# The third piece of a weight load moved to the scalar engine's DMA queue, an unused small transfer left out, and another load cut in two

## The chip, the cores and the metric

The kernel runs on one core of a Trainium2 chip. The metric is the device time of one execution in microseconds (us); the time before is the median of three runs.

## The reference

Two blocks are computed from the same input `x` (2048 tokens of 512 numbers, bf16) and mixed by a gate per token:

```python
x = A_x
g = _sigmoid((x * gate_w).sum(-1, keepdims=True))
a = _A_ref(x, A_wqkv, A_wo)
b = _B_ref(x, B_w1, B_w3, B_w2)
return g * a + (1 - g) * b

# _A_ref: linear attention, 32 heads of 16
q, k, v = qkv[0], qkv[1], qkv[2]                       # from x @ wqkv
phi = lambda t: jnp.where(t > 0, t + 1, jnp.exp(t)) + 1e-6
pq, pk = phi(q), phi(k)
kv = jnp.einsum("bhsd,bhse->bhde", pk, v)
z = jnp.einsum("bhsd->bhd", pk)
num = jnp.einsum("bhqd,bhde->bhqe", pq, kv)
den = jnp.einsum("bhqd,bhd->bhq", pq, z)[..., None] + 1e-6
o = num / den                                          # then o @ wo

# _B_ref: SwiGLU with F = 1376
h = _silu(x @ w1) * (x @ w3);  out = h @ w2
```

## The kernel before

The 2048 tokens are cut into 16 tiles of 128 (`t`), and these into four blocks of four (`tb`). The 512 input columns are cut into four pieces of 128, numbered `kc` = 0 to 3, which are the contraction steps of every projection.

**Loads.** All large loads are issued by SyncE (SP, `dq = nc.sync`) in the order of the program, each on the queue behind the one before: the first two token tiles in natural layout (`xN`, L129), the four pieces of the joined q and k weights (`wqk[:, kc, :]`, 128 rows of 2 KB each, L126), transposed loads of the tokens from tile 2 on (`xT`, L123) with natural ones between them (L141), then the weights `wr`, `w1`, `w3`, `wv`, `wo`, `w2` and `w2x` (L143 to L156). The queue of ScalarE (ACT) carries one transfer in the whole kernel: 32 bytes of each of 384 rows of `A_wqkv` into `touch` (L133), a tile that nothing reads. Ahead of it ACT runs one activation of one column (`act_pre`, L130), whose result nothing reads either; it makes ACT load its function table at the start. The pieces of code are

```python
nc.scalar.activation(out=act_pre[:], in_=warm[:, 0:1], func=ACT.Exp)
nc.scalar.dma_start(out=touch[:], in_=wqkv_r[:, 1:KC, 0:16])
for kc in range(KC):
    load_wqk(kc)
```

Every DMA also carries one of eight completion semaphores in turn; a later DMA that gets the same one waits for the DMA that had it before.

**Opening of TensorE.** The order is written out by hand (a manual schedule). 13 warm-up matmuls on a constant (L359) run while the loads are under way. Then the first two token tiles are transposed on TensorE (L365, six blocks), and VectorE and ScalarE copy the results into `xT` (L379 to L382). Then the first four projections (k and q of tiles 0 and 1) run piece by piece, as the pieces of `wqk` arrive: `kc` 0 for all four, the last two transposes, `kc` 1 for all four, and then `kc` 2 and 3 for the two k, then for the two q (all matmuls of L183).

```python
for kc in range(2):
    for n, t in (("k", 0), ("q", 0), ("k", 1), ("q", 1)):
        first_mm(n, t, kc)
    if kc == 0:
        transpose_kc(3, bank[0])
for kc in range(2, KC):
    for t in range(2):
        first_mm("k", t, kc)
```

After that come, tile by tile, the projections of q and k, `phi` (exp on ACT, two operations on VectorE), and the product of the phi'd k with the natural tokens (L231).

**The rest.** For each block the gated unit (`glu_step`, L303 and L309, with a product on VectorE at L315), in between the denominators, and the outputs: `b_part` (L492) with `w2`, `a_part` (L475), the mix on VectorE (L498) and the store (L508). `w2` is read for the first time by L492 of block 0.

Of the kernel before, what the change touches and what calls it, by code (L numbers as in the profile page):

```python
# [8 lines left out]
ACT = mybir.ActivationFunctionType  # L9
# [3 lines left out]
BF16 = mybir.dt.bfloat16  # L13
# [3 lines left out]
def kernel(  # L17
# [17 lines left out]
    nc = tc.nc  # L35
    P = nc.NUM_PARTITIONS

    Bb, S, D = A_x.shape
# [3 lines left out]
    KC = D // P  # L42
# [4 lines left out]
    FC = F // P  # L47
# [14 lines left out]
    wqkv_r = A_wqkv.rearrange("(kc d) n -> d kc n", d=P)  # L62
# [3 lines left out]
    consts = ctx.enter_context(tc.tile_pool(name="consts", bufs=1))  # L66
# [5 lines left out]
    warm = nc.const_aps.tensor(1.0, [P, 256], BF16)  # L72
# [7 lines left out]
        out=bmask[:], in_=bmask[:], pattern=[[-Dh, HPC], [0, Dh]], compare_op=ALU.is_ge,  # L80
# [3 lines left out]
        out=bmask[:], in_=bmask[:], pattern=[[Dh, HPC], [0, Dh]], compare_op=ALU.is_ge,  # L84
# [23 lines left out]
    wqk = consts.tile([P, KC, 2 * D], BF16, name="wqk")  # L108
# [6 lines left out]
    w3 = consts.tile([P, KC, F0], BF16, name="w3")  # L115
    w2 = consts.tile([P, FC, D], BF16, name="w2")
    xT = consts.tile([P, KC, S], BF16, name="xT")
    act_pre = consts.tile([P, 1], BF16, name="act_pre")
    dq = nc.sync

    def load_xT(t):
        ts = slice(t * P, (t + 1) * P)
        dq.dma_start(out=xT[:, :, ts], in_=x2d[ts, :], transpose=True)  # L123

    def load_wqk(kc):
        dq.dma_start(out=wqk[:, kc, :], in_=wqkv_r[:, kc, 0 : 2 * D])  # L126

    x_first = x2d[0 : 2 * P, :].rearrange("(p j) d -> p j d", j=2)
    dq.dma_start(out=xN[:, 0:2, :], in_=x_first)  # L129
    nc.scalar.activation(out=act_pre[:], in_=warm[:, 0:1], func=ACT.Exp)  # L130

    touch = consts.tile([P, KC - 1, 16], BF16, name="touch")
    nc.scalar.dma_start(out=touch[:], in_=wqkv_r[:, 1:KC, 0:16])  # L133
    for kc in range(KC):
        load_wqk(kc)
    natural = {3: (2, 4), 5: (4, 8), 8: (8, 16)}
    for t in range(2, NT):
        load_xT(t)
# [3 lines left out]
    with nc.allow_non_contiguous_dma(reason="gate column"):  # L142
        dq.dma_start(  # L143
            out=wr[:, :, 2 * FR : NR], in_=gate_w.rearrange("(kc d o) -> d kc o", d=P, o=1)
# [3 lines left out]
    for w, w_r, cuts in ((w1, w1_r, (0, KC)), (w3, w3_r, (0, KC))):  # L148
# [2 lines left out]
    dq.dma_start(out=wv[:], in_=wqkv_r[:, :, 2 * D : 3 * D])  # L151
    dq.dma_start(out=wo[:], in_=A_wo.rearrange("(kc d) n -> d kc n", d=P))
    w2_r = B_w2[0:F0, :].rearrange("(fc f) d -> f fc d", f=P)
    dq.dma_start(out=w2[:], in_=w2_r)
    w2x_r = B_w2[F0:F, :].rearrange("(i r) d -> i (r d)", i=RP)
    dq.dma_start(  # L156
        out=w2x[:].rearrange("p r d -> p (r d)"),
        in_=w2x_r[None].to_broadcast([TPB, RP, RG * D]),
# [442 lines left out]
```

## Time and profile before

| what | value |
|---|---|
| median of three runs | 178.73 us (178.44 to 178.74) |
| the profiled execution's own time | 177.74 us |
| its span | 176.0 us, so 1.74 us lie around it |
| TensorE busy | 171.3 us (97%) |
| VectorE, POOL, ScalarE busy | 110.5, 63.3, 59.1 us |
| chain that ended last | PE 95%, DMA 2% |
| DMA of SP's queue, ACT's queue | 28948 packets with 15.41 MB, 400 packets with 0.01 MB |

Times are counted from the start of the span. PE is TensorE's matmuls and PEld its weight loads, SPq and ACTq are the DMA issues of SyncE and ScalarE. Matmuls overlap each other, so the start of a matmul says more than its duration: four full ones take 0.86 us of the chain.

### The profile page before, as it was taken

The numbers are of one execution on the slowest core, as the hardware profiler recorded it, in microseconds if no ns is written. First come the engines' busy times: TensorE is split into PE (matmuls) and PEld (weight loads), VectorE is DVE, ScalarE is ACT, GpSimd is POOL, SyncE is SP. The second block draws the span as 40 slices with busy tenths as digits, with TensorE's granted clock in tenths as the row PEclk, the third lists the DMA queues.
The fourth block names the chain that finished last, engine by engine and source line by source line (L and its number), as shares of the span: only waits on it lengthen the run. The fifth ranks groups of instructions, "written<-read, shape, count | busy, mean of one in ns | idle before, by whom it ended". The sixth has DMA issues, their size and how long they took to land.

```text
span 176.0 us, 2668 instructions
## 1 busy us (share of the span) xinstructions
PE 171.3 (97%) x952; PEld 82.4 (47%) x969; DVE 110.5 (63%) x207; ACT 59.1 (34%) x109; POOL 63.3 (36%) x106
## 2 busy tenths in 40 slices
PE   8999999999999999999999999999999999999993
PEld 5444444444456443444444466444444444444453
DVE  0399788888764899777343477853435775344363
ACT  4364544544753533322433101224226122422000
POOL 5087656656300668586300044540000662000000
DMA  5988969997205112323200013330000233000001
GB/s 172 277 197 207 164 123 237 403 352 231 78 4 56 22 30 41 78 63 91 58 0 0 0 34 84 84 89 0 0 4 0 60 89 89 4 0 0 30 30 60
DMA packets 29360, 15.58 MB, mean 88 GB/s; under 512 B 21156, under 2 KB 27556, under 8 KB 29348
## 3 DMA queue, kind: packets, MB, share of 16 engines
q1 hardware_dynamic: 28948, 15.41, 35.1%
q8 instruction: 7, 0.11, 0.3%
q10 hardware_dynamic: 400, 0.01, 0.1%
q14 instruction: 5, 0.04, 0.1%
HBM read 8.86 MB, written 2.10 MB: 62 GB/s over the span
## 4 chain that ended last, share of the span: by engine, by line
PE 95%; DMA 2%; issue 1%; SPq 0%; DVE 0%
PE bank L303 20%; PE bank L492 20%; PE bank L309 19%; PE bank L183 16%; PE bank L231 8%; PE bank L475 8%; PE bank L245 3%; DMA wqk<-in_A_wqkv_dram 2%; PE bank L278 2%; PE bank L447 0%; SPq L129 0%; PE bank L462 0%; DVE o L498 0%; PE bank L365 0%
## 5 line engine op out<-in xcount | busy, mean ns | idle before, releaser
L315 DVE TENSOR_TENSOR hT<-bank,sg 128x512 bf16<-128x512 f32 x40 | 27.3, 682 | 31.0 <-PE bank L309 28.9
L303 PE MATMUL bank<-xT,w 128*128 128x512 bf16 x158 | 40.8, 379 | 0.2
L309 PE MATMUL bank<-xT,w 128*128 128x512 bf16 x156 | 40.5, 379 | 0.2
L314 ACT ACTIVATE sg<-bank 128x512 bf16<-128x512 f32 x40 | 23.9, 597 | 45.9 <-PE bank L303 45.9
L492 PE MATMUL bank<-w,hT 128*128 128x512 bf16 (+2 forms) x176 | 37.0, 355 | 0.5 <-issue 0.3
L337 POOL TENSOR_TENSOR pqs<-pq,rden 128x512 bf16<-128x512 bf16 x16 | 16.9, 1057 | 54.3 <-issue 46.8
L183 PE MATMUL bank<-wqk,xT 128*128 128x512 bf16 x126 | 30.2, 379 | 0.1
L215 POOL TENSOR_TENSOR zacc<-zacc,pk 128x128 f32<-128x128 f32 x56 | 23.3, 447 | 10.4 <-DVE pk L201 10.4
L492 PEld LDWEIGHTS <-hT 128*128 128x128 bf16 x180 | 16.7, 98 | 18.4 <-issue 0.8
L309 PEld LDWEIGHTS <-w 128*128 128x128 bf16 x160 | 15.7, 98 | 18.9
L303 PEld LDWEIGHTS <-w 128*128 128x128 bf16 x160 | 15.5, 98 | 18.2 <-issue 0.2
L498 DVE SCALAR_TENSOR_TENSOR o<-bank,omg_all,aga 128x512 bf16<-128x512 f32 (+2 forms) x18 | 12.4, 692 | 14.5 <-PE bank L492 11.7
L183 PEld LDWEIGHTS <-xT 128*128 128x128 bf16 x128 | 12.5, 98 | 14.9 <-issue 0.3
L322 POOL TENSOR_TENSOR pr<-pq,zb 128x512 f32<-128x512 bf16 x16 | 18.4, 1155 | 0.1
L231 PE MATMUL bank<-pk,xN 128*128 128x512 bf16 x62 | 16.3, 379 | 0.2
L475 PE MATMUL bank<-M,pqT 128*128 128x512 bf16 x61 | 15.6, 379 | 0.1
L196 ACT ACTIVATE eq<-bank 128x512 bf16<-128x512 f32 x16 | 9.4, 597 | 16.0 <-PE bank L183 14.9
L201 DVE SCALAR_TENSOR_TENSOR pk<-bank,emk 128x512 bf16<-128x512 f32 x16 | 11.1, 692 | 1.6
L196 ACT ACTIVATE ek<-bank 128x512 bf16<-128x512 f32 x16 | 9.4, 597 | 6.5 <-PE bank L183 6.5
L201 DVE SCALAR_TENSOR_TENSOR pq<-bank,emq 128x512 bf16<-128x512 f32 x16 | 11.1, 692 | 0.5
L326 DVE TENSOR_REDUCE den<-pr 128x32 f32<-128x512 f32 x16 | 10.8, 676 | 0.0
L231 PEld LDWEIGHTS <-xN 128*128 128x128 bf16 x64 | 6.3, 98 | 7.5
(54 smaller groups left out, 95.6 us busy)
## 6 DMA issues: line engine op xcount, KB each, us to landing
w<-in_B_w_dram SPq DMA_DIRECT2D x3, 1280.0 KB, 10.3
out_dram<-o SPq DMA_DIRECT2D x15, 128.0 KB, 1.9
wqk<-in_A_wqkv_dram SPq DMA_DIRECT2D x4, 256.0 KB, 3.7
xN<-in_A_x_dram SPq DMA_DIRECT2D x1, 1024.0 KB
xN<-in_A_x_dram SPq DMA_DIRECT2D x2, 256.0 KB, 2.9
xN<-in_A_x_dram SPq DMA_DIRECT2D x1, 512.0 KB, 4.2
wv<-in_A_wqkv_dram SPq DMA_DIRECT2D x1, 512.0 KB, 11.2
wo<-in_A_wo_dram SPq DMA_DIRECT2D x1, 512.0 KB, 12.2
```

What stands on the lines that cost most here:

```text
L183: nc.tensor.matmul(ps[:], lhsT=xT[:, kc, t * P : (t + 1) * P], rhs=w[:, kc, :], start=(kc == 0), stop=(kc == KC - 1),)
L196: nc.scalar.activation(out=e[:], in_=ps[:], func=ACT.Exp)
L201: nc.vector.scalar_tensor_tensor(out=dst, in0=ps[:], scalar=0.0, in1=em[:], op0=ALU.max, op1=ALU.add)
L215: nc.gpsimd.tensor_tensor(out=(zaccb if t == NT - 1 else zacc)[:, cs], in0=zacc[:, cs], in1=pk[t][:, cs], op=ALU.add,)
L231: nc.tensor.matmul(bank[kc][:], lhsT=xN[:, t, kc * P : (kc + 1) * P], rhs=pk[t][:], start=(t == 0), stop=(t == NT - 1),)
L303: nc.tensor.matmul(g_ps[:], lhsT=w1[:, kc, fs], rhs=xT[:, kc, tok], start=(kc == 0), stop=(kc == KC - 1),)
L309: nc.tensor.matmul(u_ps[:], lhsT=w3[:, kc, fs], rhs=xT[:, kc, tok], start=(kc == 0), stop=(kc == KC - 1),)
L314: nc.scalar.activation(out=sg[:], in_=g_ps[:], func=ACT.Silu)
L315: nc.vector.tensor_tensor(out=hT[tb][:, fc, :], in0=u_ps[:], in1=sg[:], op=ALU.mult)
L322: nc.gpsimd.tensor_tensor(out=pr[t][:], in0=pq[:, t, :], in1=zb[:], op=ALU.mult)
L475: nc.tensor.matmul(ps[:], lhsT=pqT[:, c, ts], rhs=M2[:, c, :], start=(c == 0), stop=(c == KC - 1),)
L492: nc.tensor.matmul(ps[:, 0 : cs.stop - cs.start], lhsT=hT[tb][:, fc, tt * P : (tt + 1) * P], rhs=w2[:, fc, cs], start=(fc == 0 and not sta ...
```

## The change

The third piece of `wqk` (`kc` = 2) is issued on ACT's queue, the other three stay on SP's. The first activation of ACT now writes its one column into that piece, `wqk[:, 2, 0:1]`, so that the transfer, which overwrites the column, has to wait for the activation. The transfer into `touch` and the tiles `act_pre` and `touch` are left out. The load of `w2` (1280 KB) becomes two of 640 KB, one behind the other on SP's queue.

```diff
-    def load_wqk(kc):
-        dq.dma_start(out=wqk[:, kc, :], in_=wqkv_r[:, kc, 0 : 2 * D])
+    def load_wqk(kc, queue):
+        queue.dma_start(out=wqk[:, kc, :], in_=wqkv_r[:, kc, 0 : 2 * D])
...
-    nc.scalar.activation(out=act_pre[:], in_=warm[:, 0:1], func=ACT.Exp)
-
-    touch = consts.tile([P, KC - 1, 16], BF16, name="touch")
-    nc.scalar.dma_start(out=touch[:], in_=wqkv_r[:, 1:KC, 0:16])
+    nc.scalar.activation(out=wqk[:, 2, 0:1], in_=warm[:, 0:1], func=ACT.Exp)
+
     for kc in range(KC):
-        load_wqk(kc)
+        load_wqk(kc, nc.scalar if kc in (2,) else dq)
...
-    dq.dma_start(out=w2[:], in_=w2_r)
+    for a, b in ((0, FC // 2), (FC // 2, FC)):
+        dq.dma_start(out=w2[:, a:b, :], in_=w2_r[:, a:b, :])
```

More of the change, by code (lines that the diff above doesn't have):

```diff
@@ L117 @@
     xT = consts.tile([P, KC, S], BF16, name="xT")
-    act_pre = consts.tile([P, 1], BF16, name="act_pre")
     dq = nc.sync
```

## The prediction

> **What bounds the kernel now.** I read the page's chain first, to see whether anything but TensorE sets the end.
>
> ```profile
> PE 171.3 (97%) x952; PEld 82.4 (47%) x969; DVE 110.5 (63%) x207; ACT 59.1 (34%) x109; POOL 63.3 (36%) x106
> PE 95%; DMA 2%; issue 1%; SPq 0%; DVE 0%
> ```
>
> TensorE is the bound, and the only load in the chain is 2% of it. So a load matters only where TensorE stands still for it. The chain in order of time, from its start, shows where that can be:
>
> ```profile
> 1.26 3.11 DMA wqk<-in_A_wqkv_dram
> 4.37 0.04 issue
> 4.41 1.02 PE bank L183 x4
> 5.43 0.11 PE bank L365 x2
> 5.54 3.60 PE bank L183 x16
> 9.14 0.65 PE bank L231 x3
> ```
>
> The first projection starts at 4.41, when piece 0 of wqk has landed (issued 1.26, 3.11 later). From there four matmuls take 0.86 (0.215 each), and 16 should take 3.45 but took 3.60: 0.15 us of stall. The timeline of the weight loads says where:
>
> ```profile
> 4.32 0.62 PEld L183 LDWEIGHTS <-xT 128*128 128x128 bf16 x4
> 5.06 0.31 PEld L365 LDWEIGHTS <-xN 128*128 128x128 bf16 x2
> 5.33 1.23 PEld L183 LDWEIGHTS <-xT 128*128 128x128 bf16 x7
> 6.83 0.74 PEld L183 LDWEIGHTS <-xT 128*128 128x128 bf16 x4 [0.27 <-issue]
> ```
>
> Counting on from 4.41: four matmuls of kc 0 to 5.27, two transposes (0.11) to 5.38, four of kc 1 to 6.25, two of kc 2 to 6.68. The first of kc 3 should start at 6.68; the loads resume at 6.83. The four pieces are issued 0.46 apart from 1.26 on, and by the landings of the four issues, asked one by one (3.1, 3.4, 3.9 and 4.1 us later), they land at 4.37, 5.1, 6.1 and 6.8. So piece 3 is 0.15 late, piece 2 has 0.2 to spare (needed at 6.25) and piece 1 has 0.2 to 0.3 (needed at 5.38). Behind 6.83 the chain is matmul after matmul; the waits listed for SP name no xT or weight load, and the tokens of tile 2 land 4.1 after 3.15, at 7.25, for use at 8.12.
>
> **The change, part by part.** PE, DVE and POOL keep their operations in their order. What moves is in the first 7 us. ACT's opening before:
>
> ```profile
> 0.80 1.28 ACT L130 ACT_TABLE_LOAD   x1 [0.80 <-PEq L585]
> 0.86 0.43 ACTq L133 DMA_DIRECT2D touch<-in_A_wqkv_dram  x1
> 2.10 0.20 ACT L130 ACTIVATE act_pre<-const-bfloat16-1.0 128x1 bf16<-128x1 bf16 x1
> 4.08 0.28 ACT L380 ACTIVATE xT<-bank 128x128 bf16<-128x128 f32 x1 [1.78 <-PE bank L365]
> ```
>
> *The activation* writes another address, the same 128x1: 0.20 us, no change. *The new wait:* the transfer of piece 2 stood on SP at 2.20; it is now issued when the activation ends, at 2.30, say 2.35, and the issue takes 0.43 as touch's did, to 2.78. Behind it on ACT waits only the copy L380, which comes at 4.08 for another reason: 1.3 us of cover, cost nothing.
>
> *SP's queue* has one issue less between pieces 1 and 3: piece 3 is issued at 2.20 instead of 2.67, and all that follows, the xT transposes and natural tokens too, 0.46 sooner until w2. Their data come no sooner by that, since they queue behind the same bytes, but none is later. The completion semaphore that each waits for moves by one place; before, none of these waits held SP, and none comes near.
>
> *Touch left out.* Its data all fell into 0.4 us, by the DMA view of 2.9 to 3.3 and of 3.3 to 3.7 us:
>
> ```profile
> q1 hardware_dynamic: 64, 0.10, 66.0%
> q10 hardware_dynamic: 400, 0.01, 56.2%
> ...
> q1 hardware_dynamic: 79, 0.16, 103.7%
> ```
>
> SP's queue (q1) had 66% of the engines beside touch (q10) and 104% after it: 0.38 x 0.4 = 0.15 us given back, by q10's own share 0.22. Everything behind touch, pieces 0 to 3, moves up by 0.15 to 0.22. Piece 0 gains nothing by it: its first weight load is at 4.32 because L379's copy ends at 3.97 + 0.29 = 4.26, and a load takes 0.1, so 4.41 stands. Piece 3 would land at 6.58 to 6.65 instead of 6.8, ahead of 6.68. That is the whole 0.15.
>
> *When do piece 2's data enter?* The trace has no full piece on ACT's queue. Bounds: SP's first transfer was issued at 0.81 and its data began between 1.5 and 2.0 (DMA share 0.06 there, 0.69 in the next half us), about 1.1 later, so 3.45; touch was issued at 0.86 and its data came at 2.9, 2.05 later, so 4.4. A piece takes 256 KB at 404 GB/s, 0.65 us. A landing comes about 0.6 after the data (xN: data to 3.0, landed when PE went on at 3.64). So without touch kc 0's data end near 3.55 and kc 1's near 4.3. Any entry between these gives the old order, 2 behind 1 and ahead of 3. Most of 3.45 to 4.4 lies there, and I take that.
>
> A rule speaks against the idea: the Trainium skill, page "DMA: Bandwidth & Descriptors", section "Issuing engines are not separate DMA queues", says that transfers of all queues run on the same 16 engines, and a second issuer saves only issue time. By that page the sum would be 0.15 as well, all of it touch's; the trace agrees that the engines are shared (66% and 56.2% in one window).
>
> *w2 in halves* costs SP one more issue:
>
> ```profile
> 30.27 3.66 SPq L154 DMA_DIRECT2D w<-in_B_w_dram  x1
> 33.98 2.95 SPq L156 DMA_DIRECT2D w2x<-in_B_w_dram  x1
> 46.10 1.21 SPq L421 DMA_TRANSPOSE zaT<-zaccb  x1
> ```
>
> Between 0.5 us (wr's and wv's issues) and 3.66 again; nearest is the small end, as 3.66 goes with the bytes and these stay. SP then stands idle from 36.93 to 46.10, so even 3.66 is covered; uncovered it would be 3.66. w2 lands 13.5 us after 30.27, at 43.8, and L492 reads it near 68. Nothing.
>
> Sum: -0.15 us. On the profiled execution 177.74 becomes 177.59. That execution lies 0.99 under the median, which I put down to nothing here, so the difference goes onto the median: 178.73 - 0.15 = 178.58. A change under 0.2% (0.36 us) is about what a measurement of this kernel, whose three runs spread over 0.30, can't tell from none. What would be late next after 6.68 is tile 2's xT, with 0.9 to spare.
>
> **The rivals.**
>
> *Piece 2 gets in piece 1's way.* If its data enter at 3.45 and take turns with piece 1's, or go ahead of them, piece 1 comes 0.65 later, less 0.15: 5.12 + 0.5 = 5.62. Then kc 3 can start at 5.62 + 0.04 + six matmuls (1.30) = 6.96, 0.13 later than now: 178.86. For it: SP's entry delay. Against: ACT's one row says 2.05.
> The same page, section "Queues, rings and completion order", has each engine go round the queues packet by packet. By that rule this rival is right if the entry is early; in touch's window q1 kept 64 packets, so some turn-taking shows, but no two large loads are seen side by side.
>
> *Piece 2 falls behind piece 3*, entering at 4.4 or later. Then it lands where the last piece does, 6.65, and kc 3 follows two matmuls later: 6.65 + 0.04 + 0.43 = 7.12, 0.29 later: 179.02.
>
> *Slower: touch was not idle.* It reads a bit of each row of pieces 1 to 3 ahead of them. If a first reading is slow, these pieces now pay for it. The price is xN's cold start: 160 and 341 GB/s in its two half us against 397 later, 0.30 + 0.07 = 0.37 us of lost data time. One such loss puts piece 3 at 6.8 - 0.15 + 0.37 and costs 0.2; from the second on it decides: two cost 0.58, so 179.31, three 0.95, 179.68. Against it: piece 0 was not touched, and ran at 397 GB/s.
>
> *Faster by more:* touch's data came while xN's last were landing. If xN too is freed by 0.22, the transposes and everything behind start that much sooner: -0.37, 178.36. Against it: touch starts at 2.9, when most of xN is through.
>
> **How the numbers follow.** Old order 0.40, xN freed too 0.18, piece 1 delayed 0.17, piece 2 last 0.10, cold rows 0.15. The likeliest gives 178.58. Faster by over 0.36: 0.11 of the 0.18, which lies on the bound, and 0.08 for spread: 0.19. Slower by over 0.36: 0.15 and 0.08 of the two delays, which reach 0.29: 0.23. Same: 0.58. The range goes from 178.36 less 0.25 of spread, 178.1, to cold rows with two losses, 179.3. It leaves out three losses and the rest of the spread.
>
> **What the changed profile would show.** ACT's issue of wqk at 2.35 with q10 carrying 0.26 MB; piece 3's issue at 2.2; no gap of the weight loads before kc 3 (6.68) and none before kc 1 (5.38) and kc 2 (6.25). A gap before kc 1 means the first rival, before kc 2 the second, both with lower GB/s between 3.5 and 6 the third; transposes before 3.65 the fourth. A change behind 10 us, in the middle or the end, would make this prediction wrong in kind, and so would a time outside the range.

## The result, and the profile after

The changed kernel takes 179.05 us (median of 18 executions, 178.55 to 181.43), the kernel before 178.41 us (18 executions, 177.75 to 178.83). The ratio is 1.0043, with a 95% interval of 1.003 to 1.0056; two executions at 181.4, with a mean granted clock of 0.991 of full, are left out of it, so it holds nothing of what they cost. So the kernel became slower by 0.43%, 0.77 us (the two medians are 0.64 apart), where the forecast had 178.58 against 178.73, 0.15 us faster. The profiled execution took 179.00 us with a span of 177.3 us; that of before took 177.74 with 176.0.

The page of the changed kernel first, its engines and the shares of its chain:

```profile
PE 172.3 (97%) x969; PEld 82.3 (46%) x969; DVE 110.1 (62%) x207; ACT 59.2 (33%) x109; POOL 63.3 (36%) x106
PE 94%; DMA 3%; ACT 1%; DVE 0%; issue 0%
```

TensorE is still the bound, but DMA has gone from 2% to 3% of the chain, and ACT, which was not among the first, has 1%. The chain of the changed kernel in order of time (start, duration, what) shows both:

```profile
2.10 0.21 ACT wqk L129
2.31 0.02 issue
2.33 5.24 DMA wqk<-in_A_wqkv_dram
7.57 0.04 issue
7.61 2.75 PE bank L181 x12
10.36 0.65 PE bank L229 x3
```

(Lines have numbers lower by two or one: L181 was L183, L125 was L126.) Before, the chain went through piece 0 and TensorE from 4.41 on. Now it goes through the function table, the activation, and piece 2 on ACT's queue: issued at 2.33, landed 5.24 later, at 7.57. The weight loads of TensorE say where it stood still:

```profile
4.28 0.55 PEld L181 LDWEIGHTS <-xT 128*128 128x128 bf16 x4
4.95 0.31 PEld L363 LDWEIGHTS <-xN 128*128 128x128 bf16 x2
5.22 0.80 PEld L181 LDWEIGHTS <-xT 128*128 128x128 bf16 x5
7.61 0.74 PEld L181 LDWEIGHTS <-xT 128*128 128x128 bf16 x4 [1.59 <-issue]
```

Before, seven loads followed one another from 5.33 and 0.27 us of gap stood ahead of kc 3. Now the gap is 1.59 us and stands ahead of kc 2, after five loads (four of kc 1 and one for kc 2 whose matmul had to wait for its data). From 7.61 the two matmuls of kc 2 take 0.43, so kc 3 starts at 8.04; before it started at 6.83. That is 1.21 us, and the spans, 176.0 and 177.3, differ by nearly the same. So nothing behind kc 3 changed the time.

The two queues in the DMA view, from 4.2 to 5.0 us and from 5.0 to 5.5 us (packets, MB, share of the 16 engines):

```profile
q1 hardware_dynamic: 116, 0.20, 69.4%
q10 hardware_dynamic: 29, 0.06, 22.6%
...
q10 hardware_dynamic: 56, 0.11, 64.4%
q1 hardware_dynamic: 33, 0.06, 36.1%
```

From 3.5 to 4.2 us q10 is not listed at all. So piece 2's data enter at 4.2 or later, 1.9 us or more after the issue, and take turns with piece 3, which SP issued ahead of them. Before, piece 2 had gone ahead of piece 3.

### The profile page after: what moved, and what is told of

Read it like the earlier page. It is cut to its first block, busy times and chain, and to the rows that moved or that the text cites. A ratio compares the mean times of both kernels' runs of the same rounds, so it can differ in the third digit from the quotient of the medians.

```text
span 177.3 us, 2685 instructions
## 1 busy us (share of the span) xinstructions
PE 172.3 (97%) x969; PEld 82.3 (46%) x969; DVE 110.1 (62%) x207; ACT 59.2 (33%) x109; POOL 63.3 (36%) x106
## 4 chain that ended last, share of the span: by engine, by line
PE 94%; DMA 3%; ACT 1%; DVE 0%; issue 0%
PE bank L490 20%; PE bank L301 20%; PE bank L307 19%; PE bank L181 15%; PE bank L473 8%; PE bank L229 8%; PE bank L243 3%; DMA wqk<-in_A_wqkv_dram 3%; PE bank L276 2%; ACT L129 1%; PE bank L445 0%; PE bank L460 0%; DVE o L496 0%; ACT wqk L129 0%
## 5 line engine op out<-in xcount | busy, mean ns | idle before, releaser
L301 PE MATMUL bank<-xT,w 128*128 128x512 bf16 x160 | 41.1, 379 | 0.0
L307 PE MATMUL bank<-xT,w 128*128 128x512 bf16 x160 | 41.1, 379 | 0.0
L490 PE MATMUL bank<-w,hT 128*128 128x512 bf16 (+2 forms) x180 | 37.5, 355 | 0.0
L181 PE MATMUL bank<-wqk,xT 128*128 128x512 bf16 x128 | 30.5, 379 | 1.3 <-DMA wqk<-in_A_wqkv_dram 1.3
L181 PEld LDWEIGHTS <-xT 128*128 128x128 bf16 x128 | 12.4, 98 | 16.2 <-issue 1.6
L473 PE MATMUL bank<-M,pqT 128*128 128x512 bf16 x64 | 16.1, 379 | 0.0
```

Of the source, the lines that this page charges most:

```text
L181: nc.tensor.matmul(ps[:], lhsT=xT[:, kc, t * P : (t + 1) * P], rhs=w[:, kc, :], start=(kc == 0), stop=(kc == KC - 1),)
L301: nc.tensor.matmul(g_ps[:], lhsT=w1[:, kc, fs], rhs=xT[:, kc, tok], start=(kc == 0), stop=(kc == KC - 1),)
L307: nc.tensor.matmul(u_ps[:], lhsT=w3[:, kc, fs], rhs=xT[:, kc, tok], start=(kc == 0), stop=(kc == KC - 1),)
L473: nc.tensor.matmul(ps[:], lhsT=pqT[:, c, ts], rhs=M2[:, c, :], start=(c == 0), stop=(c == KC - 1),)
L490: nc.tensor.matmul(ps[:, 0 : cs.stop - cs.start], lhsT=hT[tb][:, fc, tt * P : (tt + 1) * P], rhs=w2[:, fc, cs], start=(fc == 0 and not sta ...
```

## The experiments

The starts of issues are those of the timelines. The trace has 16 completions of each load, which I take for one of each of the core's 16 DMA engines; a landing is the last of them. "kc 3" is the start of its first matmul.

**The three parts by themselves.** First the unused transfer left out and nothing else:

```diff
-    touch = consts.tile([P, KC - 1, 16], BF16, name="touch")
-    nc.scalar.dma_start(out=touch[:], in_=wqkv_r[:, 1:KC, 0:16])
```

> The kernel before without the transfer into touch, all else as before. Theory Q (piece 2's late entry on ACT's queue is the whole loss): touch's 0.15 to 0.22 us of the engines come back, piece 3 lands near 6.6 instead of 6.8, the gap of the weight loads before kc 3 goes, and the time is 0 to 0.2 us under the kernel before (ratio 0.999 to 1.000). Rival C (touch warmed the rows, and the loss comes from leaving it out): pieces 1 to 3 land later than 5.1, 6.1, 6.8, and the time is 0.5 us or more over before (ratio 1.003 or more).

Measured: 178.73 us against 178.30, ratio 1.001 (0.9997 to 1.0024). The gain of 0.15 us (a ratio of 0.9992) is outside the interval. In the trace the pieces land later without touch: piece 1 at 5.58 (before 5.17), piece 2 at 6.34 (6.06), piece 3 at 7.07 (6.79). The chain has piece 1 in it, which it had not before:

```profile
1.72 3.86 DMA wqk<-in_A_wqkv_dram
5.58 0.04 issue
5.62 1.46 PE bank L181 x6
7.08 0.03 issue
7.11 2.32 PE bank L181 x10
```

Neither mechanism came out as expected: the pieces land later, as rival C has it, but the loss of 0.5 us that it expected is not there. What follows: leaving the transfer out alone gains no time. Whether it helps the pieces can't be told from one profile; more follow below.

The load of w2 in halves and nothing else:

```diff
-    dq.dma_start(out=w2[:], in_=w2_r)
+    for a, b in ((0, FC // 2), (FC // 2, FC)):
+        dq.dma_start(out=w2[:, a:b, :], in_=w2_r[:, a:b, :])
```

> The kernel before with w2 loaded in two halves, all else as before. Theory Q: no change (ratio 0.999 to 1.001), SP idle before 46 us as before. Rival W (the second issue of w2 costs): 0.5 us or more over before, with a later first L492 or a later transpose of zaccb.

Measured: 178.44 against 178.30, 1.0001 (0.9987 to 1.0015). The halves cost nothing. In the changed kernel SP issues them from 29.58 to 34.48 and then stands idle from 36.47 to 47.32:

```profile
29.58 4.90 SPq L152 DMA_DIRECT2D w<-in_B_w_dram  x2
34.52 1.95 SPq L154 DMA_DIRECT2D w2x<-in_B_w_dram  x1
47.32 1.22 SPq L419 DMA_TRANSPOSE zaT<-zaccb  x1
```

The changed kernel with w2 whole again:

```diff
-    for a, b in ((0, FC // 2), (FC // 2, FC)):
-        dq.dma_start(out=w2[:, a:b, :], in_=w2_r[:, a:b, :])
+    dq.dma_start(out=w2[:], in_=w2_r)
```

> The changed kernel with w2 in one piece: touch left out, piece 2 on ACT's queue behind the activation. Theory Q: the same loss as the changed kernel (ratio 1.003 to 1.006), piece 2 landing 4.5 to 5.5 us after its issue at 2.33, a gap of the weight loads of 1 us or more before kc 2. Rival W: back to the kernel before (0.999 to 1.001).

Measured: 179.32 against 178.30, 1.0049 (1.0033 to 1.0065), the whole loss. Piece 3 landed at 6.59, piece 2 at 7.07, kc 3 at 7.59. So the cause lies in the move, or in the move together with the missing touch.

**Without the hold.** The activation writes a tile of its own again, so ACT issues piece 2 at once:

```diff
-    nc.scalar.activation(out=wqk[:, 2, 0:1], in_=warm[:, 0:1], func=ACT.Exp)
+    nc.scalar.activation(out=act_pre[:], in_=warm[:, 0:1], func=ACT.Exp)
```

> The changed kernel with the activation writing act_pre again, so that piece 2's transfer on ACT's queue waits for nothing and is issued near 0.86. Theory Q: its data enter at about 2.8, 1.9 after the issue as in the changed kernel, ahead of piece 1; it lands near 5, piece 1 is pushed to 5.3 to 5.7, piece 3 lands near 6.6, and the time is within 0.3 us of the kernel before (ratio 0.999 to 1.0015). Rival D (two large loads on two queues disturb each other whenever they meet): some piece still lands at 7 or later and the ratio stays at 1.003 or more.

Measured: 180.31 against 178.30, 1.01 (1.0064 to 1.0135). Piece 2 was issued at 0.86 and landed at 4.72, and the last piece (3) landed at 6.83, not late at all. The loss lies elsewhere, in the first tokens. The weight loads of TensorE:

```profile
4.50 0.56 PEld L364 LDWEIGHTS <-xN 128*128 128x128 bf16 x6 [1.21 <-DMA xN<-in_A_x_dram]
...
8.16 0.76 PEld L182 LDWEIGHTS <-xT 128*128 128x128 bf16 x4 [0.28 <-issue]
```

From 2.6 on xN and piece 2 share the engines (q1 41.8%, q10 44.1% of them up to 3.6), xN comes at 4.46 instead of 3.60, TensorE stands still for 1.21 us, and then its matmuls follow each other at half rate, 0.43 us apart, until 8.2; kc 3 starts at 9.04. Neither mechanism expected for this run was what happened. The hold has a use: it keeps piece 2 behind xN. Against the held kernel, measured beside the same executions of before (1.0049), it is worth about 0.5%.

**Touch brought back, with the move.** Touch goes ahead of piece 2 on ACT's queue:

```diff
     nc.scalar.activation(out=wqk[:, 2, 0:1], in_=warm[:, 0:1], func=ACT.Exp)
+    touch = consts.tile([P, KC - 1, 16], BF16, name="touch")
+    nc.scalar.dma_start(out=touch[:], in_=wqkv_r[:, 1:KC, 0:16])
```

> The changed kernel with the transfer into touch put back, as the first one on ACT's queue; piece 2 follows it there and still waits for the activation. Theory F (the first transfer of ACT's queue is slow to start: about 2 us from issue to data, for touch at 0.86 as for piece 2 at 2.33): now piece 2 is the second one, its data enter about 1.1 us after its issue, near 3.5, it lands near 5.5, piece 1 near 5.6, and the time is within 0.3 us of the kernel before (ratio 0.999 to 1.0015). Rival G (a transfer on ACT's queue is held up by what SP's queue has in hand, whether first or not): its data enter at 4.2 or later, it lands at 7 or later, and the ratio stays at 1.003 to 1.006.

Measured: 179.43 against 178.27, 1.0074 (1.0051 to 1.0098). Touch brings nothing back: theory F falls, and G stands, though the ratio lies above its 1.006. Piece 1 is on time again (5.19), piece 3 lands at 7.32 and piece 2 last, 5.18 us after its issue at 2.33. The gap stands ahead of kc 2 as in the changed kernel:

```profile
7.56 1.39 PEld L183 LDWEIGHTS <-xT 128*128 128x128 bf16 x7 [1.28 <-issue]
```

With this run the parts make a square: neither 1.0; touch left out alone 1.001; the move alone 1.0074; both (the changed kernel, or with w2 whole) 1.0043 and 1.0049. The loss comes with the move, with touch or without it.

**Which piece, and what stands behind it.** Piece 3, the last one needed, goes to ACT's queue in the place of piece 2:

```diff
-    nc.scalar.activation(out=wqk[:, 2, 0:1], in_=warm[:, 0:1], func=ACT.Exp)
+    nc.scalar.activation(out=wqk[:, 3, 0:1], in_=warm[:, 0:1], func=ACT.Exp)
...
-        load_wqk(kc, nc.scalar if kc in (2,) else dq)
+        load_wqk(kc, nc.scalar if kc in (3,) else dq)
```

> The changed kernel with piece 3 instead of piece 2 on ACT's queue behind the activation; piece 2 is back on SP's queue behind piece 1. Theory Q (late entry on ACT's queue): piece 2 now lands near 6, and piece 3 as late as piece 2 did in the changed kernel, 7.0 to 7.6; it is needed two matmuls later and two matmuls less wait behind it, so the loss falls by 0.43 us where the clock of TensorE is up early: ratio 1.000 to 1.003. Rival: the order does not matter, ratio 1.003 to 1.006.

Measured: 179.03 against 178.27, 1.0057 (1.0033 to 1.0081). Piece 2, now on SP's queue right behind piece 1, lands at 7.48, piece 3 at 7.86, kc 3 at 7.95. One of the twelve executions took 181.04 us and is in the ratio; the other eleven have a median of 178.91, 1.0036. The order of use is right here, and the loss is not gone. So it is not only that the piece on ACT's queue is needed too early; here, too, both pieces come late.

Behind the pieces SP issues transposed loads, whose packets are small. A natural load of tiles 2 and 3 is put between them and the pieces:

```diff
-    natural = {3: (2, 4), 5: (4, 8), 8: (8, 16)}
+    natural = {5: (4, 8), 8: (8, 16)}
+    dq.dma_start(out=xN[:, 2:4, :], in_=x_t[:, 2:4, :])
```

> The changed kernel with the natural load of tiles 2 and 3 (256 KB) issued ahead of the first two transposed loads instead of behind them, so that a plain transfer, not a transposing one, stands on SP's queue behind piece 3. Theory X (transposes that start while plain packets are left on the other queue stop the engines, as in the 0.08 and 0.04 MB moved between 6 and 7 us in the changed kernel against 0.13 and 0.13 before): piece 2 lands by about 6.7, no half us before that moves under 0.12 MB, and the ratio falls to 0.999 to 1.003, tile 2's transposed tokens being up to 0.7 us later. Rival S (piece 2 is late only because it shares the engines): it lands at 7 or later as before, ratio 1.003 or more.

Measured: 179.61 against 178.27, 1.0095 (1.0059 to 1.0131); two of its eight executions took 181.4 us, and the other six have a median of 179.41, 1.0064. Pieces 1, 2 and 3 landed at 6.50, 7.52 and 7.60. The transposes are not what makes the last landing late; theory X falls. One thing that it names does go: piece 2 now completes on fifteen engines between 6.02 and 6.67 and is late on one, where in the changed kernel all sixteen completed between 7.00 and 7.57. With two natural loads ahead (tiles 2 to 7), one profile:

```diff
-    natural = {3: (2, 4), 5: (4, 8), 8: (8, 16)}
+    natural = {8: (8, 16)}
+    dq.dma_start(out=xN[:, 2:4, :], in_=x_t[:, 2:4, :])
+    dq.dma_start(out=xN[:, 4:8, :], in_=x_t[:, 4:8, :])
```

> The changed kernel with both natural loads of tiles 2 to 7 (256 and 512 KB) issued ahead of the first transposed load, so that the transposes start some 2 us later, after the pieces of wqk are done; a look for landings alone, since tile 2 will come too late for its use. Theory X (the first transposes, started on the engines that are ahead, hold up the completion of the pieces on the engines that are behind): piece 2 lands by 6.7 and the pieces spread over the engines, with no common burst of completions near 7. Rival S (sharing between the two queues alone makes piece 2 late): it lands at 7.0 or later, as in the changed kernel (7.57).

Measured: 181.47 us; pieces 1, 2, 3 at 7.64, 8.32, 8.44, later still, and a mean granted clock of 0.991. Where the clock went is seen in the windows of this kernel (stretch, its length, PE busy with the number of matmuls, granted clock, DMA share, GB/s):

```profile
3.50:5.30 1.80, 1.79 (x14) 1.00 0.86 205
5.30:7.60 2.30, 0.15 (x3) 0.96 0.97 334
7.60:9.30 1.70, 1.62 (x4) 0.50 1.94 309
9.30:11.00 1.70, 1.70 (x6) 0.55 0.79 140
```

TensorE was at full rate until 5.3 and waited 2.35 us for piece 1. The clock records of the packed trace then have half the clock from 7.41 to 10.82. From 7.68 to 10.94 eight matmuls were started, in 3.26 us, where 0.215 each makes 1.72. So in this execution the stall was paid twice, with 1.5 us on top of it. Rival S held, and the completions are spread out as theory X expected, only later and not sooner.

The same edits on the kernel before, with two natural loads and with one:

> The kernel before with both natural loads ahead of the first transposed load, as in the run before it, all four pieces on SP's queue. Theory X: piece 3 lands near 6.4 instead of 6.8 to 7.0, since its data end near 5.8 and a landing takes 0.6. Rival S: the transposes do not matter to a single queue, piece 3 lands at 6.7 to 7.0 as before.

> The kernel before with the natural load of tiles 2 and 3 ahead of the first two transposed loads. Theory X: piece 3 lands near 6.4; tile 2's transposed tokens land near 7.9 for use at 8.1, so that where the clock of TensorE is up early the gap before kc 3 goes (0.15 to 0.3 us), and otherwise nothing changes: ratio 0.998 to 1.001. Rival: the later tokens of tile 2 cost more than the gap gave, ratio over 1.002.

Measured: 179.78 us for two natural loads, of which TensorE pays for tile 2's tokens, which now come at 10.06; the pieces come at 5.05, 6.66 and 7.36, the last 0.4 later than the 6.79 to 6.99 of before, which neither mechanism had. With one natural load 178.27 against 178.40, 1.0001 (0.9989 to 1.0014), pieces at 5.19, 6.29, 6.97. In neither does piece 3 land sooner, as theory X would have it. No version measured here was faster than the kernel before.

**The same kernels again.** One profile is one execution, so both kernels were profiled again, unchanged.

> The kernel before, unchanged, for a second profile of it. Theory H (the moment at which TensorE goes from half to full rate differs from execution to execution, and the profiled 176.0 us was an early one): four projections take 0.86 or up to 1.7 us, and the span lies up to 1.6 us over 176.0 with the same landings (4.4, 5.1, 6.1, 6.8 within 0.3). Rival L (the loads differ): the span differs with the landings, and the projections take 0.86 each time.

Measured: 178.83 us, span 177.1, 1.1 us longer than the first profile of the same kernel (theory H held). Its pieces land at 5.24, 6.28 and 6.99, so a stall of the loads is not the reason. The chain of this second profile of before:

```profile
4.58 1.79 PE bank L183 x4
6.37 0.21 PE bank L365 x2
6.58 3.60 PE bank L183 x16
```

Four matmuls took 1.79 us where the first profile has 1.02: TensorE ran at half rate, 0.427 between full matmuls, until about 6.7 (in the packed trace the clock record of the full rate begins at 6.75). Then piece 3 at 6.99 is in time for a kc 3 that starts at 7.87.

> The changed kernel, for a second profile of it. Theory H with Q (late piece 2, hidden by the half-rate start of TensorE where that lasts): piece 2 lands at 7.0 to 7.6 whatever the clock; if the first projections take 0.86 for four, TensorE stands for 1 us or more before kc 2, if they take up to 1.7, for less than 0.6, and the span stays between 176.8 and 178.2. Rival: piece 2's landing differs by over 1 us from execution to execution.

> The changed kernel, a third profile. Theory M (with a piece on each queue the last pieces land later on the average, by about 0.3 us, and with much more spread, 6.6 to 7.6, than on one queue, 6.8 to 7.0; and piece 2, with two more matmuls behind it, is the last): piece 2 lands behind piece 3, between 6.6 and 7.6. Rival N (on the average the landings are as before, 6.6 to 7.0, and the first profile's 7.57 was a stray): 7.0 or earlier, no gap of the weight loads before kc 2 over 0.5.

> The kernel before, a third profile. Theory M: piece 3 lands at 6.8 to 7.0, all 16 engines within 0.2. Rival N: its landing spreads as widely as in the changed kernel, up to 7.5.

> The changed kernel, a fourth profile; the same as for the third.

Measured: the changed kernel 178.13, 179.50 and 179.26 us, the kernel before 177.95. The second profile of the changed kernel went against its forecast: piece 2 landed at 6.61 and not at 7.0 to 7.6, 1.5 us apart from the 8.09 of the third, as the rival has it. In the third and fourth, piece 2 came behind piece 3, as theory M has it, but later than its 7.6 (8.09 and 7.85). Piece 3 of the kernel before landed at 6.98 with all 16 completions within 0.13, as theory M expected. In the fastest one of the changed kernel the matmuls run at half rate up to about 5.6, the pieces land early (piece 3 at 6.34, piece 2 at 6.61), and no gap is left: its weight loads are one row,

```profile
5.85 3.17 PEld L181 LDWEIGHTS <-xT 128*128 128x128 bf16 x16
```

while the slowest waits twice, for piece 1 and for piece 2:

```profile
6.80 0.74 PEld L181 LDWEIGHTS <-xT 128*128 128x128 bf16 x4 [0.55 <-issue]
8.13 1.39 PEld L181 LDWEIGHTS <-xT 128*128 128x128 bf16 x7 [0.58 <-issue]
```

> The variant with piece 3 on ACT's queue, a second profile. Theory M: pieces 2 and 3 both land at 7.0 or later (7.48 and 7.86 in the first). Rival N: at 6.6 to 7.0.

Measured: 179.10 us, pieces 1, 2, 3 at 5.55, 7.69 and 7.58: as late as in the first profile of piece 3 on ACT's queue, as theory M expected.

> The kernel before without touch, all pieces on SP's queue, a second profile. Piece 1 landed at 5.05 to 5.24 in all seven profiles with touch, and at 4.89 to 7.64 in the ten without it, nine of which have a piece on ACT's queue as well. Theory C2 (touch makes the first reading of the pieces' rows regular): piece 1 lands outside 5.05 to 5.24 here too (5.58 in the first), piece 3 at 7.0 or later. Rival Q2 (the scatter of piece 1 is the second queue's): piece 1 lands within 0.1 of 5.0, which is 5.17 less touch's 0.15, and piece 3 at 6.6 to 6.9.

> The changed kernel with touch as the first transfer on ACT's queue, a second profile. Theory C2: piece 1 lands at 5.05 to 5.24 again. In both theories the last of pieces 2 and 3 lands at 7.2 or later (7.52 in the first), since piece 2 is still on ACT's queue.

Measured: 178.87 us without touch on one queue, pieces at 6.38, 7.05 and 7.80, all later than in the first such profile; 179.03 us with touch and the move, piece 1 at 5.54, piece 3 at 7.22, piece 2 at 7.38. Without touch, piece 1 is late a second time, as theory C2 expected. In the kernel with touch and the move C2 missed: piece 1 came at 5.54 and not at 5.05 to 5.24.

All openings side by side (us; the table leaves out the kernels with other loads or without the hold; the rows come from several chips):

| opening | piece 0 lands | piece 1 lands | last piece lands | kc 3 | span |
|---|---|---|---|---|---|
| before | 4.37 | 5.17 | 6.79 (piece 3) | 6.83 | 176.0 |
| before, second profile | 4.46 | 5.24 | 6.99 (3) | 7.87 | 177.1 |
| before, third profile | 4.53 | 5.20 | 6.98 (3) | 7.02 | 176.2 |
| before with w2 in halves | 4.52 | 5.18 | 6.98 (3) | 7.03 | 176.3 |
| after | 4.18 | 4.89 | 7.57 (2) | 8.04 | 177.3 |
| after, second profile | 4.20 | 4.98 | 6.61 (2) | 7.20 | 176.4 |
| after, third profile | 4.24 | 6.76 | 8.09 (2) | 8.56 | 177.8 |
| after, fourth profile | 4.33 | 6.45 | 7.85 (2) | 8.32 | 177.6 |
| after with w2 whole | 4.24 | 5.33 | 7.07 (2) | 7.59 | 176.9 |
| no touch, one queue | 4.29, 4.23 | 5.58, 6.38 | 7.07, 7.80 (3) | 7.11, 7.84 | 176.4, 177.1 |
| touch and the move | 4.52, 4.48 | 5.19, 5.54 | 7.52, 7.38 (2) | 7.99, 7.86 | 177.3, 177.2 |
| piece 3 on ACT's queue | 4.22, 4.29 | 5.96, 5.55 | 7.86 (3), 7.69 (2) | 7.95, 8.16 | 177.2, 177.4 |

In every row the span is the start of kc 3 plus 169.2 to 169.3 us. So the whole difference is made ahead of kc 3, and these starts can be compared in the place of times. The five profiles with the changed opening start kc 3 at 7.94 on average, the four with the opening of before at 7.19. The 0.75 us between them lies beside the 0.77 us of the timed runs; that it comes so close is luck, since the five spread over 1.36 us and the four over 1.04. On one chip (before, third profile; after, third and fourth) the order is the same.

## Why the prediction was wrong

*What bounds the kernel, and where the loads matter.* Right: TensorE from the first projection on, nothing behind kc 3. That kc 3 sets the span is now shown by every row of the table.

*The issues.* Right in size: the activation ends at 2.31, ACT issues at 2.33 for 0.37 us (forecast 2.35 and 0.43), and the copy L378 behind it starts at 4.04 (before 4.08). SP's transposes start 0.48 sooner.

*w2 in halves.* Right: 1.0001.

*Touch left out: -0.15 us.* This step failed, and it was the whole sum. It took the engines' time that touch uses for time that all the pieces behind it get back. Piece 0, which touch does not read, got it: it landed at 4.30 to 4.53, 4.46 on average, in the eight profiles with touch, and at 4.18 to 4.33, 4.25 on average, in the eleven without (the kernel without the hold is left out). So "piece 0 gains nothing" was wrong too: the chain has the first projection 0.04 behind piece 0's landing, and without touch it starts 0.18 sooner on average (4.32 and not 4.50). But pieces 1 to 3, whose rows touch reads first, did not follow (piece 1 did in two profiles of the changed kernel, 4.89 and 4.98). Without touch on one queue the last piece landed at 7.07 and 7.80 where the step had 6.58 to 6.65, and the time was 0.1% longer (-0.03 to 0.24%) and not 0.15 us shorter. From 4 to 6 us the core moved 304 and 302 GB/s in these two; in four profiles of the opening of before 351, 353, 358 and 332. The rate does not always go with touch, though: with touch it was 345 and 301 where natural loads stand ahead of the transposes, and 351 and 298 with the move. The rival "touch was not idle" had this in its mechanism, at a chance of 0.15 and with its first piece as the argument against it. Its price in landings (0.2 and more) was seen; its price in time alone was not, as far as the interval tells. Why reading 32 bytes of each row first should help the reading of the rest, no run here shows.

*Piece 2's entry: between 3.45 and 4.4, old order kept.* This step failed and made the loss. The data entered at 4.2 or later in the changed kernel's first profile, near ACT's own row (touch, 2.05 us after its issue) and not near SP's (1.1 us). That is the upper end of the stretch that the forecast had taken. What failed is that any entry in it keeps the old order: from there piece 2 went turn by turn with piece 3 and landed last, which is the rival "Piece 2 falls behind piece 3", given 0.10 and 179.02 us. Its end was right and its size was not; that its 179.02 lies beside the measured 179.05 is luck, since it was counted as 0.29 from 178.73 and the kernel before has 178.41. It had the last landing at 6.65 and two matmuls (0.43) behind it; the five profiles have the last landing at 7.57, 6.61, 8.09, 7.85 and 7.07, 7.44 on average, against 6.79 to 6.99, 6.94 on average, for one queue with touch. The 0.75 us divide so: 0.50 from the later landing, and 0.25 from what lies between it and kc 3 (0.50 on average, two matmuls and a little, against 0.25, which is 0.04 or 0.05 in three profiles and 0.88 in the one where TensorE was at half rate). The sign of the rival "Piece 2 gets in piece 1's way", a gap ahead of kc 1, stands in the third and fourth profile too; but piece 1 was as late on one queue without touch (6.38), so the second queue is not needed for it.

*The order of the pieces is not the core of it.* With piece 3 on ACT's queue, in the order of use, the loss is still 0.57% (0.36% by the medians without the execution of 181.04). What comes with two queues is that the last pieces are late on some engines. With touch kept, the third load of SP's queue completes within 0.51 us over the 16 engines in before (piece 2, 5.55 to 6.06) and within 1.97 with the move (piece 3, 5.35 to 7.32). In the changed kernel's first profile seven engines had finished piece 3 by 5.97 and the other nine came at 6.98 to 7.24. The scatter of piece 1 is another matter: it goes with the missing touch, on one queue as well (within 0.35 us in before, 4.82 to 5.17; within 1.78 without touch on one queue, 4.61 to 6.38; within 1.95 in the changed kernel's third profile, 4.81 to 6.76). That these engines fell behind is seen; why they do is open.

*The rule weighed against the trace.* The Trainium skill, page "DMA: Bandwidth & Descriptors", section "Issuing engines are not separate DMA queues", says that a second issuer saves issue time only. The runs agree that nothing else is saved, and go further: here the second issuer cost 0.43 to 0.74%.

*The 0.99 us under the median, put down to nothing.* Wrong. Part of it was a median of three executions: 18 of the same kernel have 178.41. The rest can be TensorE's rate: in the profile of before the matmuls are at full rate from 4.41 on, and in the second profile only from about 6.7. There kc 3 starts at 7.87, where its landing at 6.99 allowed 7.03, which is 0.84 of the 1.1 us by which the span is longer. So the stall of 0.15 us on which the forecast was built exists only in executions where the full rate comes early. The Trainium skill, page "TensorE: Matmul & The Clock Gate", Part 1, says that the clock opens after a free-running window of about 3.4 us, so that the moment differs by run, by 500 ns to either side. The trace agrees with the differing moment, and with the half rate (0.427 between matmuls), but not with the size: in the kernel before full rate begins at 3.96 in one profile and at 6.75 in another.

*What stays open.* The runs show that the move costs the time, and not by what mechanism the engines fall behind. How much of the late landing in the changed kernel is due to the missing touch and how much to the move can't be told from single profiles: the move with touch has 7.52 and 7.38, and both without touch 6.61 to 8.09. In time the move carries it. The profiles come from several chips, and no run here tells what a chip adds to the scatter.

## What to carry to other kernels

A load that a stalled TensorE waits for was not helped here by a second queue while the first already kept the DMA engines busy: the second queue's data came in 1.9 us after the issue, took turns with what the first queue carried, and both landed late. Before a transfer that nothing reads is called waste, leave it out by itself and look at the landing of every load behind it: here the first of them gained what the forecast said, and the others did not. And read a stall in the first microseconds from several profiles: here one profile's 0.15 us was covered by a slower TensorE in the next, and in another kernel a stall of 2.35 us brought the slower TensorE back.

## What the runs showed of the hardware that was not expected

- The moment at which TensorE goes from half to full rate lay between 3.91 and 6.75 us in eighteen profiles, by the first clock record in the packed trace of each, and at 8.19 in the kernel without the hold. In the second profile of the kernel before the late moment cost 0.84 us. The windows view gives a granted clock of 1.00 ahead of that record too; there the half rate shows only in the distance between matmuls (0.427 against 0.215).
- In one kernel, after a stall of 2.35 us in the midst of its work, TensorE fell back to half rate for 3.41 us (7.41 to 10.82), and there the granted clock of the windows does show it (0.50). After the stall of 1.59 us in the changed kernel it did not.
- While TensorE is at half rate, late loads cost less: in the second profile of before piece 3 landed at 6.99, 0.2 later than in the first, and there was no gap ahead of kc 3.
- One small read of three loads' rows (400 packets, 0.01 MB) ahead of them goes with landings of piece 1 within 5.05 to 5.24 in seven of the eight profiles that have it (5.54 in the eighth); without it, with the hold or on one queue, they lie between 4.89 and 7.64. Piece 0, whose rows it does not read, lands 0.21 us later with it.
- Two plain loads of 256 KB issued 0.06 us apart on two queues (xN and piece 2 without the hold) made the one needed first land 0.86 us later.
